# Seven weight pieces requested at the beginning in place of five, and five dummy products moved from the third attention job to the fourth

## The chip, the cores and the metric

The kernel runs on one core of one Trainium2 chip. The metric is the device time of one launch in microseconds. Before the change the median of three runs is 676.12 us (674.73 to 676.29).

## The reference

The reference is a chain of three blocks on a batch of 4, sequence 576, in float32:

```
scores = (q k^T) / 8, causal;  bias = -(cum_i - cum_j), cum = cumsum(max(s, 0))
attn   = softmax(scores + min(bias, 0));  x = attn v        # 8 heads of 64 -> 512
xk, xr = mix of x and x shifted by one row, with mu_k and mu_r
x      = sigmoid(xr w_r) * ((relu(xk w_k) ** 2) w_v)        # 512 -> 1024 -> 512
h      = gelu(x w_in), halves u and v
out    = x + (u * (w_sg layernorm(v) g_ln + b_sg)) w_out    # w_sg mixes the 576 rows
```

## The kernel before

*Numbers.* Products in full float32 accuracy are done by splitting an operand in a high and a low part (tiles ending in h and l, type fp32r) and adding three products. The weights come from DRAM as raw 64-bit words, because the host hands over the float32 arrays as they are; a piece is 128 partitions by 512 words, 512 KB. `load_words` (L96) requests one piece on SyncE's queue, `assemble` (L105) makes float32 numbers from its words (ScalarE L111, VectorE L114 and L115) and `convert` (L118) splits them (ScalarE L72 or L123, VectorE L75 or L124).

*Pieces.* The generator `conversions` (L130) walks over 20 pieces in this order: w_k (wk00, wk10, wk20, wk30, wk01, wk11, wk21, wk31), w_r (wr00 to wr30), w_v (wv00 to wv70). Each of its steps requests the piece that is AHEAD places further on and converts its own. The first AHEAD pieces are requested elsewhere, ahead of the loop: two at L249 and L250, and the others by

```
    for c in range(max(1, E1), AHEAD):
        load_words(wk, c % 4, c // 4, after=cur)
```

in a block of higher priority than the attention's own loads. The same generator serves the eight pieces of w_in much later, with nothing requested beforehand: its first step then requests the pieces 0 to AHEAD and converts the first.

*Attention.* The work is cut in jobs of two heads. Jobs 0 to 3 do the first three row blocks of the four head pairs of the first batch (`SPLIT` = 1), jobs 4 to 7 the two last row blocks, and later jobs all five. In this text the first job is n = 0. `attend` (L710) alternates: a step of `scores` of one job (a product on TensorE at L366, a fold with mask and minimum on VectorE at L381, the exponential on ScalarE at L408) with a step of `rows` of the job before (transposes at L445, copies on ScalarE at L449, products with the values at L451 and L455). The operands of queries and keys are in two tiles, used in turn; `load` (L195) fetches them for each head of a job, with one piece of the data and two rows of the running sums (L203, L206, L207), and a third tile of values (L220). All requests go out on SyncE's queue in a fixed order.

*Dummy products.* Behind each score step of the first four jobs the program puts a number of bf16 products of 384 columns, whose result nobody reads:

```
WD = (2, 1, 1, 2)
            for _ in range(WD[w.n] if w.n < len(WD) else 0):
                behind(nc.tensor.matmul(idle[:, 0:384], ones[:, 0:P], ones, start=True, stop=True), issued[0])
```

Each of these jobs has five score steps. `WT` does the same behind the transposes of the first two jobs, and 22 dummies stand at the beginning (L264).

*Order.* As long as no unit of the second block may start (L806), a loop takes a step of the attention and, on average, 0.7 steps of `conversions`. After that `moe1` leads: its products (`mm3_steps`, L687, products at L690) are the dense work of the middle of the kernel, and attention steps are woven in by a rate. What is written in the program is not yet the order on the engines: each instruction has a priority, and a planner with its own model of time puts the instructions of each engine in a fixed order. `behind` (L160) adds an ordering without a wait. The memory of the w_v pieces is that of the tiles of the running sums, so their requests stand after the storing of these sums at L324.

Of the kernel before, what the change touches and what calls it, by code (L numbers as in the profile page):

```python
# [25 lines left out]
QM = [64, 128, 128, 128, 128]  # L26
KN = [64, 192, 320, 448, 576]
PTW = 1408
C0, RATE, LEAD, AHEAD = 0.7, 1.05, 0.0, 5
FIRST = 100000  # L30
WARM = 22
SPLIT = 1
# [6 lines left out]
NS, NV = 8, 8  # L39
PACE = 3  # L40

WD = (2, 1, 1, 2)
WT = (2, 1)
GT = 150
N0 = 8
# [8 lines left out]
def block_kernel(ctx: ExitStack, tc: tile.TileContext, qkv, vb, s, w_r, w_k, w_v, mu, w_in, w_out, w_sgT, g_ln, b_sg, out):  # L54
# [105 lines left out]
    def behind(i, j):  # L160

        kind = mybir.DependencyInfo(mybir.DependencyClass.NoSync, mybir.DependencyReason.DATA)
        tc.add_manual_dep(i.ins, j.ins.name, kind)
# [207 lines left out]
    def scores(w):  # L371
# [13 lines left out]
        for j, i in w.steps[0] + w.steps[1]:  # L385
# [23 lines left out]
            exps.append(i)  # L409
            for _ in range(WD[w.n] if w.n < len(WD) else 0):  # L410
                behind(nc.tensor.matmul(idle[:, 0:384], ones[:, 0:P], ones, start=True, stop=True), issued[0])
# [786 lines left out]
```

## Time and profile before

| | |
|---|---|
| median of three runs | 676.12 us |
| the profiled execution | 676.66 us |
| its span, first to last instruction | 674.8 us |
| TensorE busy | 653.7 us, 97% |
| VectorE busy | 519.8 us, 77% |
| ScalarE busy | 426.1 us, 63% |
| GpSimd busy | 46.2 us, 7% |
| chain that ended last: TensorE | 78% |
| chain that ended last: VectorE, DMA, ScalarE | 7%, 5%, 5% |

The span is what the instructions cover; some 1.9 us of the execution lie around it. "Busy" adds the time of an engine's instructions. The chain that ended last is followed back from the last instruction, at each step to what released it.

### The profile page before, as it was taken

The page shows a single profiled execution, that of the slowest core. Times are in us where ns is not written, and L with a number is a line of the kernel's source. Part 1 is how long each engine was busy: PE and PEld are TensorE (multiplying, and loading weights), DVE is VectorE, ACT ScalarE, POOL GpSimd, SP SyncE. Part 2 cuts the span into 40 slices and gives each one's busy share as a digit, 9 for nine tenths or more (in the row PEclk, how much of TensorE's full clock was granted, in tenths as well). Part 3 has the DMA queues.
Part 4 walks back from the last instruction along what each step waited for, and adds up shares of the span by engine and source line. Part 5 has one row for each costly group of instructions (what it writes and reads, how often), then busy time and mean ns, then how long its engine had stood idle before and what let it go on. Part 6 is the DMA issues. An engine that isn't in the chain of part 4 may idle for free.

```text
span 674.8 us, 12820 instructions
## 1 busy us (share of the span) xinstructions
PE 653.7 (97%) x4590; PEld 612.4 (91%) x4590; DVE 519.8 (77%) x1329; ACT 426.1 (63%) x1014; POOL 46.2 (7%) x95
## 2 busy tenths in 40 slices
PE   7898999899999999999999999999999999999998
PEld 4666989798889999999999999999998998998997
DVE  7798867988889997878996659727488786867856
ACT  6788977779768977958986849526354423233222
POOL 6010000011100100100110100000000000000002
PEclk9899999999999999999999999999999999999999
DMA  7899332353433234233211074103131150320222
GB/s 202 256 271 273 111 96 82 102 161 94 112 109 118 84 87 130 80 94 120 79 44 65 11 262 146 54 36 125 53 123 36 53 160 1 106 71 0 89 80 71
DMA packets 41399, 71.65 MB, mean 106 GB/s; under 512 B 8244, under 2 KB 23968, under 8 KB 41304
## 3 DMA queue, kind: packets, MB, share of 16 engines
q1 hardware_dynamic: 41336, 70.84, 34.9%
q8 instruction: 36, 0.59, 0.4%
q14 instruction: 27, 0.22, 0.1%
HBM read 56.29 MB, written 10.19 MB: 99 GB/s over the span
## 4 chain that ended last, share of the span: by engine, by line
PE 78%; DVE 7%; DMA 5%; ACT 5%; issue 2%; POOL 1%; SPq 1%; DVEq 0%; ACTq 0%; POOLq 0%
PE m L690 30%; PE pu L703 8%; PE ps L1000 4%; PE av L539 3%; PE p L1000 3%; PE t L554 3%; PE pg L963 3%; PE pg L964 2%; PE pg L962 2%; PE av L455 2%; PE pv L894 2%; PE pv L893 2%; PE pv L892 2%; PE s L366 2%; PE s L369 2%
## 5 line engine op out<-in xcount | busy, mean ns | idle before, releaser
L408 ACT ACTIVATE pr<-pr,nm 128x448 f32<-128x448 f32 (+4 forms) x144 | 84.9, 592 | 18.3 <-DVE nm L381 17.9
L690 PE MATMUL m<-xh,wk 128*128 128x288 f32 x512 | 85.8, 301 | 0.3 <-ACT kf L650 0.3
L690 PE MATMUL m<-kh,wv 128*128 128x288 f32 x512 | 79.4, 297 | 0.0
L690 PEld LDWEIGHTS m<-xh,wk 128*128 128x128 f32 x512 | 73.2, 189 | 2.9 <-ACT kf L650 0.8
L381 DVE CUSTOM_DVE_ANT_0 pr<-s,mask 128x320 f32<-128x320 f32 (+3 forms) x128 | 60.6, 476 | 18.9 <-PE s L369 11.5
L690 PEld LDWEIGHTS m<-kh,wv 128*128 128x128 f32 x512 | 71.6, 188 | 0.5
L75 DVE TENSOR_TENSOR xl<-xf,xh 128x288 fp32r<-128x288 f32 (+1 forms) x80 | 40.7, 524 | 12.0 <-ACT xh L828 8.8
L690 PE MATMUL m<-xl,wk 128*128 128x288 f32 x256 | 47.7, 299 | 0.0
L557 ACT CAST pth<-t 128x512 fp32r<-128x512 f32 (+1 forms) x72 | 37.9, 533 | 14.1 <-PE t L554 13.3
L558 DVE TENSOR_TENSOR ptl<-t,pth 128x512 fp32r<-128x512 f32 (+1 forms) x72 | 43.6, 612 | 3.8 <-ACT pth L557 3.5
L368 PE MATMUL s<-qk 128*128 128x288 f32 (+4 forms) x132 | 42.0, 320 | 2.1 <-DVE nh L381 1.0
L690 PE MATMUL m<-kl,wv 128*128 128x288 f32 x256 | 43.7, 298 | 0.0
L622 ACT ACTIVATE xf<-xt,mu 128x288 f32<-128x288 f32 x64 | 33.1, 535 | 15.0 <-POOL xt L520 10.3
L690 PE MATMUL m<-xh,wr 128*128 128x288 f32 x256 | 41.8, 300 | 0.0
L554 PE MATMUL t<-early,pr 128*128 128x128 f32 x252 | 39.0, 273 | 2.6 <-DVE ptl L558 2.6
L369 PE MATMUL s<-qk 68*128 68x288 f32 (+4 forms) x132 | 40.2, 309 | 0.3 <-DMA qk<-gate_d 0.3
L628 DVE SCALAR_TENSOR_TENSOR xf<-xt,mu_sb,xf 128x288 f32<-128x288 f32 x64 | 32.3, 513 | 9.4 <-ACT xf L622 9.1
L703 PE MATMUL pu<-xh,wi 128*128 128x288 f32 x256 | 39.4, 295 | 0.0
L690 PEld LDWEIGHTS m<-xl,wk 128*128 128x128 f32 x256 | 38.7, 188 | 0.6 <-issue 0.2
L650 ACT ACTIVATE kf<-m 128x288 f32<-128x288 f32 x64 | 26.2, 412 | 19.3 <-PE m L690 18.8
L963 PE MATMUL pg<-wg,vh 128*128 128x288 f32 x128 | 37.8, 295 | 0.0
L690 PEld LDWEIGHTS m<-kl,wv 128*128 128x128 f32 x256 | 37.4, 189 | 0.4
(284 smaller groups left out, 1711.9 us busy)
## 6 DMA issues: line engine op xcount, KB each, us to landing
qld<-qkv SPq DMA_DIRECT2D x24, 288.0 KB
kld<-qkv SPq DMA_DIRECT2D x24, 288.0 KB
x_d<-rt SPq DMA_DIRECT2D x8, 576.0 KB
xf<-x_d SPq DMA_DIRECT2D x8, 576.0 KB
vld<-qkv SPq DMA_DIRECT2D x24, 160.0 KB
qk<-qk SPq DMA_DIRECT2D x24, 144.0 KB
ot<-x_d SPq DMA_DIRECT2D x24, 144.0 KB
outT<-ot SPq DMA_DIRECT2D x24, 144.0 KB
```

What stands on the lines that cost most here:

```text
L75: (nc.gpsimd if pick(engines) == "P" else nc.vector).tensor_tensor(dst, a, b.bitcast(F32), ALU.subtract)
L368: nc.tensor.matmul(dst, qk[0][:, 0, qs], qk[0][:, 1, ks], start=True, stop=False)
L369: issued[0] = nc.tensor.matmul(dst, qk[1][0 : D + 4, 0, qs], qk[1][0 : D + 4, 1, ks], start=False, stop=True)
L381: nc.vector.tensor_tensor_reduce(out=dst, in0=src, in1=msk, scale=-0.125, scalar=first, op0=ALU.add, op1=ALU.min, accum_out=acc)
L408: i = nc.scalar.activation(dst, dst, AF.Exp, bias=nm[:, col : col + 1], scale=-1.0, accum_out=acc)
L554: issued[0] = nc.tensor.transpose(bank[:, o : o + P], x, ident)
L557: nc.scalar.copy(pth[:, cols], bank[:, 0:o])
L558: nc.vector.tensor_tensor(ptl[:, cols], bank[:, 0:o], pth[:, cols].bitcast(F32), ALU.subtract)
L690: i = nc.tensor.matmul(dst, w(x, c, m), xx[:, c], start=(n + c == 0), stop=(n == 2 and c == w.nk - 1))
L703: nc.tensor.matmul(dst, w(x, c, m), xx[:, c], start=(n + c == 0), stop=(n == 2 and c == w.nk - 1))
L963: nc.tensor.matmul(pg[:, 0:HD], vh[k][:, ds], wg[1][k][:, hs], start=False, stop=False)
L1000: nc.tensor.matmul(dst, wq[a][:, y, c, ms], x[z][c], start=(n == 0), stop=(n % 6 == 5), skip_group_check=(n >= 6))
```

## The change

Three lines of constants change, of which one constant (RATE) is read nowhere.

```diff
-C0, RATE, LEAD, AHEAD = 0.7, 1.05, 0.0, 5
+C0, RATE, LEAD, AHEAD = 0.7, 0.95, 0.0, 7
-WD = (2, 1, 1, 2)
+WD = (2, 1, 0, 3)
```

With AHEAD at 7 the loop at L309 requests wk20, wk30, wk01, wk11 and wk21 in place of wk20, wk30 and wk01. Each step of `conversions` then requests a piece that is seven places further on in place of five; of w_in the first step requests all eight pieces in place of six, and the second and third have none left to request. With the new WD the third job (n = 2) has no dummy product behind its five score steps, in place of one, and the fourth (n = 3) has three, in place of two. The count of dummies stays at 30 behind score steps.

## Rows read from the trace of the kernel before

**Rows 1.** windows by stage: length, busy (count) of PE, PEld, DVE, ACT, POOL, clock, DMA share, GB/s

```profile
20.00:60.00 40.00, 34.13 (x190) 23.58 (x190) 32.35 (x98) 31.76 (x75) 2.77 (x5) 0.96 0.94 281
60.00:200.00 140.00, 133.71 (x949) 122.30 (x949) 116.22 (x314) 111.87 (x272) 8.21 (x15) 1.00 0.39 111
...
sum 674.80, PE 653.74 PEld 612.45 DVE 519.80 ACT 426.13 POOL 46.24; mean PE 163.44 PEld 153.11 DVE 129.95 ACT 106.53 POOL 11.56
```

**Rows 2.** TensorE in order of time, opening: start, length, instruction, [idle before <- releaser]

```profile
13.36 1.10 PE L366 MATMUL s<-qk 128*128 128x320 f32 x4 [1.46 <-POOL qk L168]
...
21.27 0.81 PE L366 MATMUL s<-qk 128*128 128x320 f32 x2
...
24.80 0.49 PE L366 MATMUL s<-qk 128*128 128x128 f32 x2
25.13 0.33 PE L411 MATMUL warm<-early 128*128 128x384 bf16 x1
27.98 0.49 PE L451 MATMUL av<-vb,p 128*128 128x130 f32 x2 [2.53 <-ACT p L449]
...
55.19 0.66 PE L445 MATMUL t<-early,pr 128*128 128x128 f32 x4 [1.36 <-ACT xt L484]
```

**Rows 3.** ScalarE in order of time: first conversion steps that waited for a piece

```profile
26.80 0.66 ACT L111 ACTIVATE cvt<-wk11w 128x512 f32<-128x512 f32 x1 [2.38 <-DMA wk11w<-w_k]
...
51.72 0.68 ACT L111 ACTIVATE cvt<-wv00w 128x512 f32<-128x512 f32 x1 [1.06 <-DMA wv00w<-w_v]
...
54.08 0.66 ACT L111 ACTIVATE cvt<-wv10w 128x512 f32<-128x512 f32 x1 [0.64 <-DMA wv10w<-w_v]
```

**Rows 4.** SyncE's requests in order of time: start, length of issue, tile

```profile
12.93 0.43 SPq L100 DMA_DIRECT2D wk01w<-w_k  x1
13.46 0.66 SPq L203 DMA_DIRECT2D qk<-qkv  x1
...
17.78 0.21 SPq L207 DMA_DIRECT2D qk<-cur_d  x1
...
20.14 0.60 SPq L203 DMA_DIRECT2D qk<-qkv  x1
...
21.59 0.36 SPq L100 DMA_DIRECT2D wk11w<-w_k  x1
```

**Rows 5.** windows of the opening, columns as in rows 1

```profile
13.10:15.00 1.90, 1.64 (x9) 1.29 (x10) 0.49 (x2) 1.05 (x3) 1.60 (x7) 1.00 0.98 328
...
20.60:22.50 1.90, 1.90 (x12) 1.21 (x12) 1.90 (x7) 1.71 (x5) 0.00 (x0) 1.00 0.43 118
...
28.10:30.00 1.90, 1.90 (x13) 1.90 (x14) 1.54 (x5) 1.90 (x7) 0.00 (x0) 0.70 0.89 278
30.00:31.90 1.90, 1.90 (x8) 1.32 (x8) 0.48 (x3) 1.19 (x4) 0.22 (x1) 0.50 1.03 319
31.90:33.80 1.90, 1.90 (x9) 1.18 (x8) 1.69 (x7) 0.98 (x3) 0.00 (x0) 0.90 1.03 260
...
41.00:45.00 4.00, 4.00 (x23) 2.63 (x23) 3.98 (x14) 3.33 (x10) 0.61 (x1) 1.00 0.74 192
```

**Rows 6.** what SyncE's requests waited for: us, times, longest; 11 to 18, 18 to 22

```profile
SPq L207 <- DMA wk30w<-w_k: 1.1, 1, 1.1
...
SPq L203 <- DMA wk01w<-w_k: 2.1, 1, 2.1
```

**Rows 7.** windows: 17 value products at full clock, columns as in rows 1

```profile
38.07:39.80 1.73, 1.73 (x17) 1.73 (x17) 1.65 (x7) 1.73 (x6) 0.00 (x0) 1.00 1.06 254
```

**Rows 8.** TensorE in order of time, fourth job: two dummies and the next instruction

```profile
33.82 0.49 PE L411 MATMUL warm<-early 128*128 128x384 bf16 x2
34.14 0.38 PE L483 MATMUL t<-early,avt 128*128 128x128 f32 x2
```

**Rows 9.** the w_in stage: first request behind the eight pieces; a window

```profile
399.94 0.36 SPq L825 DMA_DIRECT2D xf<-x_d  x1
...
400.00:420.00 20.00, 20.00 (x146) 19.66 (x145) 19.77 (x44) 17.94 (x40) 0.00 (x0) 1.00 0.54 180
```

## The prediction

> **What bounds the kernel now.** I read the totals first, then the windows by stage, then TensorE's order of time in the early stages, then what SyncE's requests wait for. In the windows TensorE is busy for 653.74 of 674.80 us [rows 1], so at most 21 us of idle time can be won. They also say where: 5.87 us of idle TensorE between 20 and 60 us (40.00 less 34.13) and 6.29 us between 60 and 200 [rows 1]. The edit touches the opening. There the same windows show DMA at a share of 0.94, against 0.39 in the next one: the opening is a race of transfers, and behind it the kernel is a dense stream of products.
>
> In TensorE's order of time the longest gap of the opening is plain: a dummy product starts at 25.13, the next real product at 27.98, after 2.53 us of idleness that ended when ScalarE had copied a transposed block [rows 2]. ScalarE was late because it works in order and stood before that copy at the first step of converting the sixth weight piece (wk11), waiting 2.38 us for it to land [rows 3]. That piece was requested at 21.59 [rows 4], after all operands of the third job and half of those of the fourth. The gap has a second price: TensorE's granted clock, 1.00 before, is 0.70, 0.50 and 0.90 on average in the three windows from 28.1 to 33.8 [rows 5]. The levels being 1.2 and 2.4 GHz, these 1.9 us windows lost 0.57, 0.95 and 0.19 us, 1.71 us together.
>
> **The change, part by part.** *The sixth and seventh piece are requested in the opening block.* Their two requests come to stand behind that of the fifth, at 12.93, and ahead of the operands of the third job, requested at 13.46 [rows 4]. A piece takes about 2.36 us in a full queue: a later request waited for the fourth piece (wk30), another for the fifth (wk01) [rows 6], and they went out at 17.78 and 20.14 [rows 4]. So the two land at about 22.5 and 24.9, in place of the sixth landing just before 26.80. ScalarE reached that conversion at 24.42 (26.80 less 2.38), so its wait goes, and with it TensorE's: 2.53 us. If what stands there next is only partly ready, the gain is less; bounds 0 and 2.53.
>
> The half clock: an idle stretch of 1.46 us before 13.36 [rows 2] left the clock at 1.00 [rows 5]; the one of 2.53 us was followed by the fall. If no gap above 1.5 us is left, the 1.71 us come back too. Bounds: all of it, or none, or as much again lost if a longer gap arises; I take all, as the nearer row for a remaining gap near 1 us is the one of 1.46.
>
> *What it pushes back.* The third job's first operands landed between 20.14, when the fifth piece was down, and 21.27, when their first product ran [rows 2, 4]. With two pieces of 2.36 us ahead of them they come at 24.9 to 26.0, say 25.4, 4.1 us later. Does TensorE have other work until then? From 21.27 to the end of the last dummy at 25.46 are 4.19 us. In them stand three score steps of the third job, 0.81 + 0.49 + 0.49 us (the middle one like the last), and three of its dummies at 0.16 [rows 2]: without these about 1.9 us remain, to 23.2. The 17 products of attention times values behind the old gap need nothing of the third job and take 1.73 us at full clock [rows 7]: 24.9. In the best order the new wait is thus 0.5 us or nothing; in the worst, with the third job's score at the head of TensorE's order, it is the full 4.1 us. The planner chooses the order and the trace does not show it. I take 1.0 us, near the low end, because the older job's work is what the steps alternate with and the nearest gap left in the opening is the one of 1.46; I keep 0 and 4.1 as the ends.
>
> *The dummies.* Two of them started at 33.82 and the next instruction at 34.14 [rows 8], so one is 0.16 us. The third job loses five. Three stood just ahead of the idle gap (the last at 25.13, rows 2), where they cost nothing; two fell after it, 0.33 us at full clock. The fourth job gains five, 0.81 us, in a stretch where TensorE had little air: the window of its product group is 1.73 busy of 1.73 [rows 7]. Net 0.5 us lost; bounds -0.3 and +0.8.
>
> *The later weights.* All requests now run two conversions further ahead, so the transfers' free time is used earlier: a share of 0.57 in the 1.90 us from 20.60, and of 0.26 in the 4.00 us from 41 [rows 5], 1.08 + 1.04 = 2.1 us. In the same opening ScalarE also waits for wv00 at 51.72 and wv10 at 54.08 (1.06 and 0.64 us, rows 3), and TensorE stands idle 1.36 us before 55.19 behind it [rows 2]. Summing the parts above, the chain arrives there 2.53 + 1.71 - 1.0 - 0.5 = 2.7 us sooner, the pieces only 2.1 us sooner; 0.6 us of new waiting is the result, of which I count 0.4, as ScalarE's wait has been passed on to TensorE at 1.36 of 1.70 or less. Bounds: all 1.36 us of that gap vanish, or 2.7 us are given back.
>
> *The input weights of the third stage* use the same constant: eight requests at once instead of six and then two. Here nothing is to be had or lost: the first transfer behind them is requested at 399.94, after all eight already, and TensorE is busy 20.00 of 20.00 us from 400 to 420 [rows 9]. The constant RATE is read nowhere. From 60 to 200 us the written order will come out somewhat differently because the planner re-times everything; of the 6.29 us of idleness there I let 1.5 us go either way, and 0 into the sum.
>
> **The sum**, against the profiled execution (676.66 us, a span of 674.8 and 1.9 around it): -2.53 - 1.71 + 1.0 + 0.5 + 0.4 = -2.3, so 674.3. The median of the runs shown is 676.12, 0.54 below that execution; the forecast for a median is 673.8 us.
>
> **A rule weighed.** In the trace, the fourth and fifth pieces went down one after the other, 2.36 us apart, and requests behind them waited [rows 4, 6]. The Trainium skill, DMA: Bandwidth & Descriptors, section Queues, rings and completion order, says that requests of one issuing engine share one row of rings and that each DMA engine takes descriptors in ring order. By that rule a prefetch cannot slip past or be passed; the trace agrees as far as its 2.36 us spacing goes.
>
> **The rivals.**
> *The prefetch blocks the third job.* Mechanism: the score product that needs the late operands stands first in TensorE's order, so TensorE idles from about 21.3 to 25.4. For it: operands and pieces share one queue, and the work that could fill the time is alternated with scores. Against it: about 4 us of other work exists. The old gap goes (-2.53), 4.1 comes; the clock falls as before, after an idle stretch longer than the one that made it fall, and with no dummies in the third job it could stay down as long again (0 to +1.7); dummies +0.5; the later wait for wv vanishes in part (-0.7). Between +1.4 and +3.1, and 677.5 to 679.2. It decides once the new wait exceeds the old gap of 2.53 us.
> The rule above speaks for this rival: in ring order nothing of the third job passes the two pieces.
>
> *The gain is given back at wv.* The same bytes pass the same queue, and wv00 may not come sooner than the 1.08 us of air at 20.60 to 22.50. Then ScalarE waits at 51 to 54 us for what was gained before it: gain 1.1 us or, with the dummies in full, 0.6; time 675.0 to 675.5. For it: a share of 0.94 over 40 us. Against it: the air at 41 to 45.
>
> *The pieces don't go ahead.* The planner may put the third job's operands first after all, as requests become ready in its own model. Then nothing is pushed back, the sixth piece still lands some 2.5 us sooner, and the sum loses its +1.0 and perhaps the wv term: -3.3 to -3.7, 672.4 to 672.8. Against it: the opening block has the higher priority, and the third to fifth pieces did go ahead of these operands [rows 4].
>
> **How the numbers follow.** This kernel's measurement can tell about 0.3% from no change, 2.0 us, so faster means below 674.1 and slower above 678.1. Forecast 0.42; pieces not ahead 0.11; given back 0.27; blocked 0.20. The forecast's own range is 672.3 to 674.9, from the bounds of 0 to 2.0 for the new wait and the 1.5 us of re-planning; its upper end is within 0.3%, so 0.34 of its 0.42 counts as faster. With the 0.11 and 0.01 of the given-back case that is 0.46. Of the blocked case the milder fifth stays within 0.3%: slower 0.16, and the same is the rest, 0.38. For 8 in 10 the range runs from 671.6 to 677.9, which takes in the two gaining cases, the given-back case and the milder half of the blocked one.
>
> **What would show it.** In the changed profile: wk11 and wk21 requested in a row with wk01 near 13 us; no wait of ScalarE's first conversion step for wk11; TensorE's gap at 25 to 28 gone or below 1.5 us, and its granted clock at 1.00 up to 34 us; the third job's first score at 24 to 26 us; waits for wv00 and wv10 within 0.6 us of the old ones. I am wrong if an idle gap of 2.5 us or more opens at 21 to 26, if the half clock stays, if the waits for wv grow by 2 us, or if idleness from 60 to 200 us changes by more than 1.5.

## The result, and the profile after

The changed kernel takes 680.2 us (median of 6 runs, 678.83 to 681.84) where the kernel before takes 675.42 (6 runs, 673.0 to 676.29). The ratio is 1.0079, with a 95% interval of 1.0057 to 1.010: slower. The forecast was 673.8, its range ended at 677.9.

The profiled execution of the changed kernel took 680.27 us with a span of 678.5, 3.7 more than before. The windows by stage (columns as in rows 1) tell what it is made of:

```profile
20.00:60.00 40.00, 33.92 (x181) 24.64 (x180) 31.77 (x97) 31.97 (x75) 3.42 (x5) 0.88 0.90 259
60.00:200.00 140.00, 131.72 (x934) 120.64 (x933) 111.58 (x303) 108.76 (x262) 7.97 (x14) 1.00 0.37 114
...
sum 678.50, PE 656.10 PEld 615.32 DVE 519.94 ACT 426.74 POOL 47.83; mean PE 164.03 PEld 153.83 DVE 129.99 ACT 106.69 POOL 11.96
```

TensorE is busy 2.36 us longer than in [rows 1] (656.10 against 653.74) though it does the same products: they run slower, as the granted clock from 20 to 60 us is 0.88 against 0.96. And it idles 1.34 us longer. Of that, the stretch from 60 to 200 brings 1.99 (8.28 against 6.29), the one from 20 to 60 brings 0.21 (6.08 against 5.87), and the first 20 us take 0.87 back.

TensorE in order of time (start, length, instruction, [idle before <- releaser]), opening:

```profile
20.62 0.43 PE L471 MATMUL t<-pth,vb 128*64 128x128 f32 x2
24.17 1.41 PE L366 MATMUL s<-qk 128*128 128x320 f32 x2 [3.12 <-DMA qk<-qkv]
25.37 0.63 PE L483 MATMUL t<-early,avt 128*128 128x128 f32 x2
25.79 1.06 PE L445 MATMUL t<-early,pr 128*128 128x128 f32 x4
...
55.28 1.09 PE L445 MATMUL t<-early,pr 128*128 128x128 f32 x8 [2.08 <-ACT xt L472]
```

The gap of 2.53 us at 27.98 [rows 2] is gone. In its place stands one of 3.12 at 24.17: the third job's first score waits for its operands, and the older job's work that needs nothing of them (L483, L445) comes behind it in TensorE's fixed order. The gap at 55 us has grown from 1.36 to 2.08.

ScalarE in order of time:

```profile
22.69 0.65 ACT L111 ACTIVATE cvt<-wk11w 128x512 f32<-128x512 f32 x1
26.04 0.38 ACT L484 COPY xt<-t 128x256 f32<-128x256 f32 x1 [2.70 <-PE t L483]
...
49.26 0.68 ACT L111 ACTIVATE cvt<-wv00w 128x512 f32<-128x512 f32 x1
...
53.81 0.66 ACT L111 ACTIVATE cvt<-wv10w 128x512 f32<-128x512 f32 x1 [2.03 <-DMA wv10w<-w_v]
```

The wait of 2.38 for wk11 [rows 3] is gone: the conversion runs at 22.69 without one. But ScalarE then idles 2.70 behind TensorE's new gap, and its wait for wv10 has grown from 0.64 to 2.03. Its wait for wv00, 1.06 before [rows 3], is gone in this profile (49.26), so the two waits together have grown by 0.33 us only, from 1.70 to 2.03. TensorE's gap behind them has grown more, by 0.72. SyncE's requests in order of time (start, length of issue, tile):

```profile
13.03 0.43 SPq L100 DMA_DIRECT2D wk01w<-w_k  x1
13.50 0.43 SPq L100 DMA_DIRECT2D wk11w<-w_k  x1
13.98 0.60 SPq L100 DMA_DIRECT2D wk21w<-w_k  x1
14.67 0.83 SPq L203 DMA_DIRECT2D qk<-qkv  x1
...
33.63 0.37 SPq L324 DMA_DIRECT2D gate_d<-gt  x1
34.10 0.60 SPq L203 DMA_DIRECT2D qk<-qkv  x1
...
38.09 0.36 SPq L220 DMA_DIRECT2D vb<-vb  x1
38.49 0.43 SPq L324 DMA_DIRECT2D gate_d<-gt  x1
...
43.74 0.36 SPq L100 DMA_DIRECT2D wv00w<-w_v  x1
44.23 0.60 SPq L203 DMA_DIRECT2D qk<-qkv  x1
...
46.49 0.35 SPq L100 DMA_DIRECT2D wv10w<-w_v  x1
```

The two pieces stand ahead of the third job's operands, which are now requested at 14.67 in place of 13.46 [rows 4]. Two things further down were not foreseen. The two storings of the running sums (L324), on which the memory of the w_v pieces depends, are torn apart by a fetch of the fifth job (L203 to L220). And wv10 is requested 2.75 us behind wv00, with a fetch between them; in the kernel before it is 0.81 us.

The clock in windows of the changed kernel (the value before the DMA share):

```profile
23.00:30.00 7.00, 5.83 (x21) 4.63 (x22) 2.20 (x6) 3.22 (x8) 0.37 (x1) 0.51 0.61 164
30.00:50.00 20.00, 19.50 (x121) 14.14 (x120) 19.23 (x64) 18.25 (x45) 2.62 (x4) 1.00 0.93 275
...
57.00:61.00 4.00, 4.00 (x17) 3.31 (x17) 3.70 (x11) 4.00 (x10) 0.00 (x0) 0.57 0.97 274
```

TensorE runs at the lower of its two levels, 1.2 GHz, for nearly all of 23 to 30 us, and again from 57 to 61, behind the gap at 55. Before there was one such stretch, inside 28.1 to 33.8 [rows 5]. The Trainium skill, TensorE: Matmul & The Clock Gate, section HAM oscillation — how this bites in real kernels, says that waits for DMA between bursts of products can send the clock back to its lower level. The trace agrees here for both gaps: that of 3.12 us waits for a transfer, that of 2.08 for ScalarE, which had waited for one. But a run below has such a gap of 2.78 us and no fall.

Last, the stretch where most of the new idleness lies. TensorE between 80 and 140 us, its waits of over 0.5 us, with two neighbours of the second:

```profile
90.73 1.02 PE L366 MATMUL s<-qk 128*128 128x448 f32 x2 [0.59 <-DVE nh L381]
...
98.57 0.51 PE L368 MATMUL s<-qk 128*128 128x288 f32 x2
100.28 0.50 PE L369 MATMUL s<-qk 68*128 68x288 f32 x2 [1.19 <-DMA qk<-gate_d]
...
100.84 1.28 PE L445 MATMUL t<-early,pr 128*128 128x128 f32 x8
...
133.17 0.38 PE L539 MATMUL av<-ptl,vv 128*128 128x256 f32 x1 [1.21 <-DVE ptl L558]
```

In the same order of time the kernel before has one such wait:

```profile
128.73 0.47 PE L368 MATMUL s<-qk 128*128 128x448 f32 x1 [1.04 <-DVE nh L381]
```

Over the 60 us TensorE idles 4.51 us after the change and 2.40 before.

### The profile page after: what moved, and what is told of

It reads as the page before. It is cut to its first block, busy times and chain, and to the rows that moved or that the text cites. A ratio compares the mean times of both kernels' runs of the same rounds, so it can differ in the third digit from the quotient of the medians.

```text
span 678.5 us, 12820 instructions
## 1 busy us (share of the span) xinstructions
PE 656.1 (97%) x4590; PEld 615.3 (91%) x4590; DVE 519.9 (77%) x1329; ACT 426.7 (63%) x1014; POOL 47.8 (7%) x95
## 3 DMA queue, kind: packets, MB, share of 16 engines
q1 hardware_dynamic: 41336, 70.84, 33.8%
## 4 chain that ended last, share of the span: by engine, by line
PE 77%; DVE 9%; ACT 6%; DMA 5%; issue 3%; SPq 1%; POOL 0%; DVEq 0%; ACTq 0%
PE m L690 30%; PE pu L703 7%; PE ps L1000 4%; PE p L1000 3%; PE s L366 3%; PE av L539 3%; PE t L554 3%; PE pg L963 3%; PE pg L964 2%; PE pg L962 2%; PE pv L894 2%; PE pv L892 2%; PE pv L893 2%; PE s L369 2%; ACT pr L408 2%
## 5 line engine op out<-in xcount | busy, mean ns | idle before, releaser
L369 PE MATMUL s<-qk 68*128 68x288 f32 (+4 forms) x132 | 40.2, 309 | 1.2 <-DMA qk<-gate_d 1.2
```

Of the source, the lines that this page charges most:

```text
L369: issued[0] = nc.tensor.matmul(dst, qk[1][0 : D + 4, 0, qs], qk[1][0 : D + 4, 1, ks], start=False, stop=True)
```

## The experiments

Each kernel was timed beside the kernel before on the same chip; ratios are to that, with 95% intervals. Each run also has a mean granted clock for the whole execution, and these differ between runs of one and the same program. In the 94 runs of the kernel before that stand beside the experiments, those at 0.997 or more took 673.4 to 674.0 us on average (three chips), those at 0.992 or less 676.8 to 677.3; straight lines through the three sets have slopes of 450 to 525 us per unit of clock. I use 500: 0.001 of clock is 0.5 us. It splits a difference in a part that goes by the clock and a rest. The split is rough: within the 6 to 12 runs of each of the other kernels such lines have slopes from 30 to 750. And the mean clock is not that of the opening alone: eight of the fourteen profiles show 0.97 in the window from 80 to 140 or from 140 to 200 us.

First question: which of the two edits does it?

**Seven pieces, the old dummies.** From the kernel before:

```diff
-C0, RATE, LEAD, AHEAD = 0.7, 1.05, 0.0, 5
+C0, RATE, LEAD, AHEAD = 0.7, 0.95, 0.0, 7
```

> The changed kernel with the old dummies (2, 1, 1, 2): seven pieces at the beginning alone. Theory A (the two pieces stand ahead of the third job's operands; TensorE waits 3.1 us for them, its clock falls, and the rest follows): the wait of about 3 us at 21 to 24 us stays and the time stays near the changed kernel's, 679 to 681 us. Theory B (the moved dummies: none in the third job to bring the clock back, three in the fourth in the way): the half clock lasts 3.4 us in place of 6.8, and the time comes down by 1.7 to 2.5 us, to 677.5 to 678.5. Theory C (what is written differently by the planner between 60 and 200 us costs 2 us, whichever constant is touched): 677 to 679, with idleness from 60 to 200 us near 8 us.

Measured 674.51 us against 674.51: 0.9997 [0.998, 1.0015], at the same mean clock (0.9961 both). Run again on another chip it gave 0.9994 [0.9973, 1.0016]:

> Seven pieces at the beginning with the old dummies, once more. Its order of requests already has the sums stored ahead of that fetch. By the theory it is within 0.2% of the kernel before and 4 to 6 us below the changed kernel. If seven pieces cost something by themselves that the other chip hid, it lies 0.3% or more above the kernel before.

Its TensorE in order of time, opening:

```profile
23.55 0.87 PE L366 MATMUL s<-qk 128*128 128x320 f32 x2 [2.25 <-DMA qk<-qkv]
```

The gap for wk11 is exchanged for one for the third job's operands of 2.25 us (3.10 in the second profile). All three theories had expected 677 us or more. So the exchange itself is worth nothing, and the new wait alone doesn't make the changed kernel slower. In this kernel's SyncE order the storings stand together and the w_v requests come 3 to 5 us sooner than in the changed one:

```profile
31.36 1.61 SPq L324 DMA_DIRECT2D gate_d<-gt  x2
...
40.57 0.36 SPq L100 DMA_DIRECT2D wv00w<-w_v  x1
41.61 0.36 SPq L100 DMA_DIRECT2D wv10w<-w_v  x1
```

ScalarE doesn't wait for either piece in it.

**The dummies alone.** From the kernel before:

```diff
-WD = (2, 1, 1, 2)
+WD = (2, 1, 0, 3)
```

> The kernel before with the new dummies (2, 1, 0, 3) alone. Theory A: no third-job wait for operands, the gap of 2.5 us at 25 to 28 us as before, time within 1 us of before (674.5 to 676.5). Theory B: the half clock behind that gap lasts about 6.8 us in place of 3.4, and with the dummies of the fourth job 2 to 3 us are lost: 677.5 to 678.5. Theory C: 676.5 to 678, idleness from 60 to 200 us 7 to 8 us.

Measured 677.22 us: 1.0051 [1.003, 1.0071]. The mean clock of its runs is 0.9915 against 0.9961, which is 2.3 us; the difference is 2.7 us in medians and 3.2 in means. Split in its two halves, on another chip, with `WD = (2, 1, 0, 2)` and `WD = (2, 1, 1, 3)`:

> The kernel before with no dummies in the third job and two in the fourth as before: (2, 1, 0, 2), five dummies fewer. If the loss of the dummies alone comes from the third job, in which TensorE then has too little to do around the gap for wk11 to get its clock back, it is in this kernel: mean granted clock near 0.992 in place of 0.996, 677 to 678 us. If it comes from the three dummies in the fourth job, this kernel is at 674 to 675 us (0.8 us of dummies fewer than before).

> The kernel before with one dummy in the third job as before and three in the fourth: (2, 1, 1, 3), five dummies more. If the loss comes from the third job, this costs only its 5 x 0.16 = 0.8 us or less: 674.5 to 675.5 us, mean clock 0.996. If the dummies of the fourth job stand in the way, 677 us or more at an unchanged clock.

Without the third job's dummies: 676.08, 1.0002 [0.998, 1.0024], clock 0.9921 against 0.9942. With three in the fourth: 676.77, 1.0021 [1.0001, 1.004], clock 0.995. Taking five products away gains no time that can be seen, while the mean clock is lower; the interval of some 1.5 us either way is wider than the 0.8 us that they last. Adding five costs 0.8 us, with an interval from 0.1 to 2.7. The halves add up to 0.9 of the 2.7 us, so they don't settle the price of the whole. The first one's windows (columns as in rows 1):

```profile
24.00:28.00 4.00, 0.88 (x4) 0.69 (x5) 1.41 (x8) 1.57 (x4) 0.00 (x0) 0.91 0.95 291
28.00:31.00 3.00, 3.00 (x16) 3.00 (x16) 1.66 (x3) 2.81 (x9) 0.22 (x1) 0.50 0.96 309
31.00:34.50 3.50, 3.50 (x10) 2.07 (x10) 1.94 (x9) 0.69 (x3) 0.00 (x0) 0.55 1.02 221
```

The gap for wk11 is 3.00 us there, and the half clock lasts to 34 us, where before it lasted to about 32 [rows 5]. That the missing dummies did this is not shown by one profile: the kernel before with an ordering more (below) has the old dummies, and its clock is 0.50 and 0.62 in the last two of these windows.

**The new dummies with five pieces at the beginning.** From the changed kernel, with `conversions` given its distance as an argument, so that all later requests keep theirs of seven:

```diff
...
-    for c in range(max(1, E1), AHEAD):
+    for c in range(max(1, E1), 5):
...
-        loaded=AHEAD,
+        loaded=5, ahead=7,
...
```

> The changed kernel with wk11 and wk21 taken out of the opening block: the third job's operands are requested first, the pieces behind them; the distance of seven and the new dummies stay. Theory A: the wait of 3.1 us for the operands is gone, the gap for wk11 at 25 to 28 us is back, and the time is that of before within 1 us, 674.5 to 676.5. Theory B: still slow, 677.5 to 679, since the dummies are the new ones. Theory C: 677 to 679, with idleness from 60 to 200 us near 8 us.

Measured 677.53: 1.0038 [1.0017, 1.006], clock 0.9919. The gap for wk11 is back (2.81 us at 27.38), and from 60 to 200 us TensorE idles 5.99 us, so the third theory, with near 8, does not hold for it. The three kernels that have that gap and no dummy in the third job have mean clocks of 0.9915, 0.9919 and 0.9921; the kernel before 0.9942 to 0.9961. So with five pieces the kernels without dummies in the third job ran at a lower mean clock; at which place they lose it is not shown.

**Seven pieces and two dummies per step in the third job.** From the kernel before:

```diff
-C0, RATE, LEAD, AHEAD = 0.7, 1.05, 0.0, 5
+C0, RATE, LEAD, AHEAD = 0.7, 0.95, 0.0, 7
-WD = (2, 1, 1, 2)
+WD = (2, 1, 2, 2)
```

> Seven pieces at the beginning with two dummies per score step in the third job and two in the fourth: (2, 1, 2, 2). If the clock around the third job decides, more dummies there help: mean clock 0.997 or more and 672.5 to 674 us, below the kernel before. If the half clock comes from the wait for operands alone (2 to 3 us), whatever follows it, the clock is as with one dummy (0.996) and the time 674.5 to 675.5.

Measured 676.69: 1.0014 [0.9993, 1.0036], clock 0.9958. That is not a proven loss, and a second dummy does not raise the clock above the 0.9961 and 0.9947 with one.

**A bridge of dummies over the new wait.** In the changed kernel, 18 more bf16 products ahead of the third job's first score:

```diff
...
+                    for _ in range(18 if w.n == 2 and (j, i) == w.steps[0][0] else 0):
+                        bridge = nc.tensor.matmul(idle[:, 0:384], ones[:, 0:P], ones, start=True, stop=True)
+                        behind(bridge, issued[0])
                     product(w, pt[:, 0 : n1 - n0], qs, slice(k0 + n0, k0 + n1))
+                    if bridge is not None:
+                        behind(issued[0], bridge)
...
```

> The changed kernel with 18 more dummy products (18 x 0.16 = 2.9 us) on TensorE just ahead of the third job's first score, that is in the gap in which it waits for the operands. They need nothing and end about when the operands land. Theory A says part of the loss is the clock: granted clock 1.00 from 20 to 30 us in place of 0.66, and the time 1.5 to 2.5 us below the changed kernel, 677.5 to 678.7, with the operands still landing at 24 us. Theory B says the same of the clock. If the clock is not what costs, the time stays at 680; if the dummies stand in the way, 681 or more.

Measured 684.07: 1.0137 [1.0102, 1.0171]. The question of the clock was not answered, because the planner made another order of it. It put the older job's products with the values ahead of the bridge, so the bridge and the third job's first score run later than the 24.17 of the changed kernel. The clock did stay at 1.00 up to 34 us, but a longer wait follows in TensorE's order:

```profile
26.76 3.09 PE L402 MATMUL warm<-early 128*128 128x384 bf16 x18
29.68 0.70 PE L366 MATMUL s<-qk 128*128 128x320 f32 x2
...
35.80 0.80 PE L366 MATMUL s<-qk 128*128 128x128 f32 x2 [4.31 <-DVE nm L381]
```

Second question: seven pieces alone cost nothing, the dummies alone 2.7 us, together 4.8. What is the rest?

**The w_v requests sooner.** The changed kernel with one ordering more, on SyncE's queue alone: the second storing of the sums goes ahead of the fifth job's second fetch. The orders of the other engines are those of the changed kernel.

```diff
...
-            if n:
+            if n and ((n, j) != (4, 1) or not behind(small[0], stored[0])):
...
-        nc.sync.dma_start(gate_d[p : p + 16], gtf[p : p + 16])
+        stored[0] = nc.sync.dma_start(gate_d[p : p + 16], gtf[p : p + 16])
...
```

> The changed kernel with one ordering more on SyncE's queue: the second half of the running sums is stored before the operands of the fifth job's second head are fetched, so that the pieces of w_v can be requested sooner. The orders of the other engines are those of the changed kernel, word for word. If what the two edits cost together beyond the dummies alone (680.2 against 677.5) is ScalarE's wait of 2.0 us for wv10 and the second stretch of half clock behind it, both go and the time is 676.5 to 678.5. If it is the different order of the products between 60 and 200 us, the time stays at 679.5 to 681.

Measured 676.2: 1.0016 [0.9995, 1.0037], clock 0.996. Its SyncE in order of time:

```profile
36.10 0.31 SPq L324 DMA_DIRECT2D gate_d<-gt  x1
36.51 0.37 SPq L220 DMA_DIRECT2D vb<-vb  x1
36.92 3.06 SPq L203 DMA_DIRECT2D qk<-qkv  x2
...
40.87 0.36 SPq L100 DMA_DIRECT2D wv00w<-w_v  x1
41.28 0.42 SPq L100 DMA_DIRECT2D wv10w<-w_v  x1
```

The two w_v requests are in a row again. Its windows, and its TensorE at the wait for the operands:

```profile
20.00:30.00 10.00, 6.96 (x45) 5.12 (x44) 7.68 (x26) 7.99 (x20) 0.97 (x2) 1.00 0.71 205
...
50.00:60.00 10.00, 9.39 (x64) 7.54 (x64) 9.38 (x24) 9.80 (x22) 0.00 (x0) 1.00 1.03 299
```

```profile
23.51 0.78 PE L366 MATMUL s<-qk 128*128 128x320 f32 x2 [2.78 <-DMA qk<-qkv]
```

From 50 to 60 us TensorE idles 0.61 us where the changed kernel idles 2.46 (its window there is 7.54 busy), and no second fall of the clock follows. The wait for the operands is still there, in this profile without any fall behind it.

**The same on one chip with the changed kernel.** To have both against the same runs, the changed kernel and this one were run again, and the same ordering was put in the kernel before:

> The changed kernel once more, beside the next three on one chip. Both theories: 0.6 to 1.0% above the kernel before, as the first time.

> The changed kernel with the storing of the sums ahead of the fifth job's second fetch, once more. If the late requests for w_v are what the two edits cost together, it is 3 to 4.5 us below the changed kernel on the same chip, and within 0.35% of the kernel before. If the first reading was the chip's, it is level with the changed kernel.

> The kernel before with the same extra ordering: sums stored ahead of the fifth job's second fetch. Its waits for wv00 and wv10 are 1.1 and 0.6 us, and the storing moves up by four requests and one piece only, so by the theory it gains 0 to 1.5 us: 0.9975 to 1.000 of the kernel before. If a later fetch of the fifth job's operands matters more, it is slower by up to 2 us.

| kernel | median us | ratio to before (675.95) | mean us | mean clock |
|---|---|---|---|---|
| before | 675.95 | | 675.52 | 0.9950 |
| changed | 680.13 | 1.007 [1.0043, 1.0097] | 680.25 | 0.9923 |
| changed, w_v sooner | 677.05 | 1.0027 [1.0006, 1.0047] | 677.05 | 0.9960 |
| seven pieces, old dummies | 675.03 | 0.9994 [0.9973, 1.0016] | 675.62 | 0.9947 |
| before, with the ordering | 676.15 | 1.0007 [0.9988, 1.0027] | 676.15 | 0.9940 |

The one ordering on SyncE is worth 3.1 us to the changed kernel and nothing to the kernel before, whose storings stood together anyway. The second profile of the changed kernel shows the same fault as the first: wv00 and wv10 are requested at 45.52 and 48.80. TensorE in order of time, and the window behind:

```profile
53.52 0.62 PE L471 MATMUL t<-pth,vb 128*64 128x128 f32 x2 [1.77 <-ACT xt L472]
56.66 1.97 PE L445 MATMUL t<-early,pr 128*128 128x128 f32 x8 [1.83 <-ACT xt L472]
```

```profile
54.00:60.00 6.00, 4.17 (x14) 2.60 (x14) 3.70 (x10) 4.49 (x10) 0.00 (x0) 0.50 1.01 250
```

**Read from the traces, not tried: 80 to 140 us.** What the ordering doesn't win back lies there. TensorE's idleness in these 60 us, by profile: 4.51 and 4.28 us in the two of the changed kernel, 4.46 and 4.23 in the two with w_v sooner, 4.51 with seven pieces and two dummies; 2.40 before, 2.65 and 1.96 with seven pieces alone, 2.49, 2.25 and 2.25 with the dummies or a half of them alone, 2.26 with the new dummies and five pieces, 2.38 in the kernel before with the ordering. The kernels of the first group all have seven pieces and other dummies than before, and all have the same three waits of about 0.6, 1.1 to 1.2 and 1.2 us. One kernel with seven pieces and the new dummies is not in it: the bridge kernel idles 2.96 us here and has two of the three waits; over the whole stretch from 60 to 200 us it does lose as much as the group (8.54). One of the three waits can be followed. With seven pieces alone, TensorE's order has a block of dense products between the two scores:

```profile
94.69 1.28 PE L445 MATMUL t<-early,pr 128*128 128x128 f32 x8
95.73 1.04 PE L690 MATMUL m<-xh,wr 128*128 128x288 f32 x6
96.61 0.29 PE L368 MATMUL s<-qk 128*128 128x288 f32 x1
97.30 0.50 PE L369 MATMUL s<-qk 68*128 68x288 f32 x2 [0.40 <-DMA qk<-gate_d]
```

In the changed kernel that block and the transposes stand behind the L369 product at 100.28, which waits 1.19 us for an operand that is fetched just ahead of it in both (requested at 99.56, and at 95.92 with seven pieces alone). No kernel was made that changes only this.

**The account**, in means on the one chip: the changed kernel is 4.7 us above the kernel before. The clock is 0.0027 lower: 1.4 us. The idleness at 80 to 140 is about 1.9 us larger (4.28 less 2.40). 1.4 us remain. The ordering takes back 3.2 us, of which 1.8 are clock (0.0037) and 1.4 are not, so the remainder and the lower clock both go with the late w_v pieces. The profiles agree with the first of these two: from 20 to 60 us TensorE idles 6.08 and 7.58 us in the two of the changed kernel and 4.63 and 4.78 in the two with the ordering. (A comparison with the profile of the kernel before doesn't show this remainder: from 50 to 60 us that profile idles 2.37 us, hardly less than the changed kernel's 2.46 and 3.60. It is one of the slower runs of its kernel, see below.) What is left above the kernel before, 1.5 us, is the 1.9 at 80 to 140 less 0.5 for a clock 0.001 higher. The terms close to 0.1 us, though each is good to some 0.5. Shown by experiment are the nought of the seven pieces and the 3.1 us of the ordering; the split by clock, and the 1.9 us at 80 to 140, are argued.

## Why the prediction was wrong

*Right:* the requests of wk11 and wk21 stand in a row near 13.5 us; ScalarE's wait for wk11 and the gap of 2.53 us are gone; the operands arrive 2.9 us later (24.17 against 21.27; 4.1 was forecast). The operands, requested behind the two pieces, also came in behind them: SyncE's request at 23.64 had waited for wk21, and the score that waits for the operands started at 24.17. So far the ring order that the prediction weighed agrees. Its conclusion that a prefetch cannot be passed goes further than an order of taking, and no run here tests it.

*The step that failed first* is "I take 1.0 us" for the new wait. It measured 3.12, and 2.25 to 3.22 in the other kernels with the seven pieces and no bridge. The prediction knew both ends and that the planner's order was not shown; it reasoned that the older job's work would fill the time because steps alternate. But the order within a step is fixed before the run: the score is placed ahead, and a wait at it stops all that stands behind. With it fell the half clock's return: the sum had -1.71 for it, yet a stretch at half clock followed the new gap as it had followed the old. These two terms alone turn the -2.8 that the sum gave to the seven pieces into 0.1 (with a wait of 2.25) to 1.0 (with 3.12), and about zero was measured for them. The mechanism is that of the rival "The prefetch blocks the third job", which had a loss of 1.4 to 3.1 with the dummies (0.5); seven pieces alone show none.

*The second* is the term for w_v, 0.4 us, built on pieces that come 2.1 us sooner by spare transfer time. The distance did not decide it. The place of two requests in SyncE's order did: wv00 was requested at 43.74, against 45.46 before, and wv10 at 46.49, against 46.27, while ScalarE was ready for it sooner (51.78 against 53.44). With its half clock it cost 3.2 us in means (the experiment with the ordering). The rival "given back at wv" named the place, but as a matter of the queue's bytes; its 675.5 us counted neither that the clock would fall again here nor the idleness further on.

*The third* is the nought for re-planning between 60 and 200 us, with 1.5 either way. It measured 2.0 in the changed kernel, and 2.0 to 2.5 in the others with seven pieces and other dummies than before; seven pieces alone have 1.0 and 0.6 more than before, which the times of that kernel don't show.

*The dummies* were priced at 0.16 us each, +0.5 together. Alone they cost 2.7 (3.2 in means), of which 2.3 go with a lower mean clock, a term that the sum did not have for them. How they lower it is open. In the changed kernel this price is not seen: with w_v sooner its clock is 0.996.

*The input weights* show no loss: idleness from 200 us to the end is 4.5 us in both.

The base was off, too. At its clock of 0.997 the profiled execution of the kernel before took 676.66 us, where its later runs at 0.997 or more took 673.4 to 674.0 on average and 675.4 at most. A single profile was taken as typical, and it was one of the slower ones. What varies between runs beside the clock is not settled.

## What to carry to other kernels

A prefetch put ahead of operands in one queue moves a wait, and what that is worth depends on what stands behind the waiting instruction in its engine's fixed order; where that order is not known, the term should be taken at its bad end. When a planner orders the whole program, a small edit in the opening can reorder requests and products far from it: compare each queue's order around scarce memory (here the storings that free the w_v pieces) before pricing anything. And take a kernel's clock and time from several runs, as one profile may be a few microseconds off what is usual.

## What the runs showed of the hardware

- The same program's runs differ in mean granted clock, from 0.989 to 1.000 in the 94 runs of the kernel before, and by 5 us or so with it.
- In these profiles the length of a gap in TensorE's work alone doesn't tell whether the clock falls behind it. A wait of 2.78 us had no fall (the kernel with w_v sooner, clock 1.00 from 20 to 60); the same kernel's second profile waits 3.22 us at the same place and has 0.72 and 0.50 in the two windows from 24 to 28 us; with seven pieces alone a wait of only 2.25 us has 0.53 and 0.62 there.
- Five bf16 dummy products of 0.16 us each, three ahead of a gap and two behind it, could be taken out without a gain that can be seen (ratio 1.0002 [0.998, 1.0024]); the mean clock without them was 0.9921 in 12 runs, against 0.9942 in 35. That the clock is what ate the gain is not shown.
